# One written order for all engines of an attention and MoE kernel, with the first unit's MoE in plain float32

## The chip, the cores and the metric

The kernel runs on one core of a Trainium2 chip. Its engines each work through a queue of their own in order: TensorE (PE; PEld is its weight load), VectorE (DVE), ScalarE (ACT), GpSimd (POOL) and SyncE (SP), which here issues all transfers. The metric is the device time of one execution in microseconds; the median of three runs of the kernel before is 644.41 us.

## The reference

The reference computes a gated linear attention with a complex decay and puts its output through a dense feed-forward block with a special gate, called MoE in the code. Cut to what matters:

```python
mag = sqrt(a_re**2 + a_im**2);  scale = minimum(mag, 0.999) / (mag + 1e-6)
for t in range(768):                       # batch 4, heads 8, head_dim 48
    S = (a_re + 1j*a_im)[t] * scale[t] * S + k[t] v[t]^T     # complex state, per head
    y[t] = q[t] @ real(S)
x = y as (3072 tokens, 384)
h = x @ w_in                               # (384, 2048)
out = (h * tanh(softplus(h))) @ w_out      # (2048, 384)
```

All inputs are float32 but the two weights, which arrive as float64 and are handed to the kernel as 64-bit integers.

## The kernel before

**Units.** The 3072 tokens are cut into 12 units of 256 tokens (a batch has three), and each unit into two chunks of 128. A unit passes through three parts.

The *elementwise* part (`ew_steps`) loads a_re, a_im, q, k and v and turns the decay into a magnitude and a phase: logarithms and exponentials (function table "natural_log_exp"), arctangent, sine and cosine (table "trig"), two prefix sums, the growth of q and k, and their rotation. Units 0 and 1 are worked in halves. The rotated q and k are sent through the DMA queues into another layout, the tile `T` (24 transfers for a unit, called relays).

The *attention* part (`attn_steps`) does for each chunk and each group of four heads: transposes of k (`pkn`, L462), products of k and q (`pa`, L470), masked on VectorE (`am`, L473), the output (`ypsum`, L486, with the chunk's own values and with the old state), and the state's update (`pd`, L502; addition L508; fade on POOL, L510, for unit 0 on VectorE). The output is moved into the layout `xf` by four transfers. These matmuls are plain float32.

The *MoE* part (`moe_steps`) works in eight pairs of 128-column blocks. For pair j, `mm1` makes `ph` = x w_in (L548), then a chain runs: exponential (ScalarE), cap (VectorE, L553), square, logarithm, exponential (ScalarE), gate (VectorE, L558), the split of the gate's result `g` into `gh` and `gl` (L157, L158), and `mm2` adds g w_out to `po` (L576). In float32 precision this is done with float32r products: each operand is split into a high and a low part, and a product is three matmuls (high x high, low x high, high x low). There are three `ph` buffers, so TensorE can be three pairs ahead of the gate.

**Weights.** `win` and `wout` convert the float64 words in 24 pieces of 512 words: ScalarE scales the low word (L123 on `raw` and `wraw`), VectorE shifts and joins the high word (L190, L194), POOL adds the carry (L199), and the split makes high and low parts (L157, L158). All this must be done for a piece before any product uses it. Since the weights come late, the MoE of units 0 and 1 is halved: pairs 0 to 3 of unit 0, pairs 0 to 3 of unit 1, then pairs 4 to 7 of each. The first half's sums go to a buffer in memory (`held`) and come back.

**Order.** Each step is put on a time line by tables of constants (`EW`, `AT`, `WP`, `LD` and others) and the framework's scheduler orders the instructions by the resulting priorities and by its own time simulation. Table loads of ScalarE are kept together by added dependencies (`with_trig`): one excursion to the trig table for units 0 and 1, two for each later unit. Thirty bf16 matmuls on `junk` keep TensorE occupied before the first products (L434).

Of the kernel before, what the change touches and what calls it, by code (L numbers as in the profile page):

```python
# [33 lines left out]
NJ = 3  # L34
DJ = D // NJ
W = TU + NCH
NPAIR = DF // (2 * P)
LAG = 3
TB = 3
HACT, HMOD = 2, 3  # L40
LDVE, LMOD = 6, 6
GACT = 0
GATE = -1
GRP = 2
RG, QG, GN = 3, 1, 0
SQ0, SORD, CGA, CGN, CGD, ACTG = 1, 0, 3, 3, 0, 0
YDVE = []
RQ = [(), ()]
LG, WG = 12, 12
W1 = 0  # L50
ADDV = 12
CLAMPP, MAGP = 0, 0
ROTU = 2
ROTP = [2]
TREE = 1
WXB, WRB, WI = 1, 2, 512
FIN0 = -2.63
FS = 0.0
TRUNC = 0
AFTERX = 0  # L60
NUN = 12
SUBP = 0
MULP = 0
LONG = 2
WIDE = 1
WREP, WREP2, WK = 18, 12, -8.6
FAST = [0, 1]
EW = [(-16.11, -10.98), (-12.73, -8.83), (-13.6, -11.78), (-17.88, -11.79), (-16.43, -10.6)]
AT = [(-7.62, -4.55), (-3.79, -0.81), (-8.05, -2.82), (-8.41, -3.06), (-10.49, -2.73)]
WP = [(-7.98, -3.4), (-2.82, 2.46), (1.94, 7.2), (9.3, 9.35)]  # L70
WS = [-3.58, -1.77, 0.11, 1.02]
ES = [3.85, -0.77, -2.02, 1.25]
TS = [0.08, -1.31, 2.46, -0.05]
MB = [-1.35, -0.14]
WL1 = -0.98
RB = 2
XB = 2
LD = [(-17.86, -17.24, -16.49), (-18.78, -19.85, -19.81), (-17.97, -17.71, -17.6), (-21.23, -15.07, -17.56), (-24.18, -15.85, -17.38)]
WL = 512
# [3 lines left out]
TWOPI_LO = 6.283185  # L83


@with_exitstack
def tile_kernel(ctx, tc, q, k, v, are, aim, w_in, w_out, out):
# [8 lines left out]
    ps = ctx.enter_context(tc.tile_pool(name="ps", bufs=1, space=PSUM))  # L96

# [17 lines left out]

    NOSYNC = mybir.DependencyInfo(mybir.DependencyClass.NoSync, mybir.DependencyReason.DATA)
    fence = {"last": None, "since": []}

    def after(ins, prev):
        tc.add_manual_dep(ins.ins, prev.ins.name, NOSYNC, reason="activation table order")  # L120

    def act(out, in_, func, **kw):
        ins = nc.scalar.activation(out, in_, func, **kw)  # L123
        if func in (AF.Exp, AF.Ln):
            if fence["last"] is not None:
                after(ins, fence["last"])
            fence["since"].append(ins)
        return ins

    def act_set(name, prevs):  # L130
        ins = nc.scalar.preload_act_table_set(name)  # L131
        for p in prevs:
            after(ins, p)
        return ins

    def with_trig(*parts):
        prev = act_set("trig_and_small", fence["since"] + [fence["last"]])
        for part in parts:
            if callable(part):
                part()  # L140
                continue
            for out, in_, func, kw in part:
                ins = nc.scalar.activation(out, in_, func, **kw)
                after(ins, prev)
                trig.append(ins)
                prev = ins
        fence["last"] = act_set("natural_log_exp_and_others", [prev])
        fence["since"] = []

    fence["last"] = act_set("natural_log_exp_and_others", [])  # L150

    wi = {p: wts.tile([P, NPAIR, NJ, 256], F32R, name=f"wi{p}") for p in "HL"}
    wo = {}
    raw_in = [wts.tile([P, NJ * DF // 2], I64, tag=f"wo{i}", name=f"raw{i}") for i in range(2)]

    def split(src, h, lo, heng, leng):
        heng(h, src)  # L157
        leng(out=lo, in0=src, in1=h.bitcast(F32), op=ALU.subtract)  # L158

# [3 lines left out]
    relayed = []  # L163
    placed = []
    relayed1 = []
    qloads = []
    turned = []
    converted = []
    trig = []
    rotated = []  # L170

    def load_win(half):
        def f():
            for o in range(0, NJ * DF // 2, WL):
                ins = nc.sync.dma_start(raw_in[half][:, o:o + WL],
                                        w_in[:, half * NJ * DF // 2 + o:half * NJ * DF // 2 + o + WL])
                if half:
                    after(ins, placed[3] if o // WL >= RG else qloads[-1] if QG else relayed[-1])
        return f

    def convert(n, raw, dst, ws, raw_is_in=False):
        u = raw.bitcast(U32).rearrange("p (n two) -> p n two", two=2)
        lo, hi = u[:, :, 0], u[:, :, 1]
        if not TRUNC:
            ins = act(lo.bitcast(I32), lo, AF.Copy, scale=2.0 ** -29)
            if CGA < 9:
                after(ins, trig[0 if len(converted) < CGN else CGA])
            converted.append(ins)
        x = me.tile([P, ws], U32, tag="wx", name="wx", bufs=WXB)
        first = nc.vector.tensor_scalar(x, hi, 3, 0x3FFFFFF8, ALU.logical_shift_left, ALU.bitwise_and)  # L190
        after(first, turned[1] if n < GN and raw_is_in else turned[GATE])
        if CGD:
            after(first, rotated[CGD - 1])
        nc.vector.scalar_tensor_tensor(hi, hi, 0xC0000000, x, ALU.bitwise_and, ALU.bitwise_or)  # L194
        if TRUNC:
            nc.vector.scalar_tensor_tensor(hi, lo, 29, hi, ALU.logical_shift_right, ALU.bitwise_or)
        else:
            hi, lo = hi.bitcast(I32), lo.bitcast(I32)
            nc.gpsimd.tensor_tensor(hi, hi, lo, ALU.add)  # L199
        split(hi.bitcast(F32), dst[0], dst[1], nc.scalar.copy if n % HMOD < HACT else nc.vector.tensor_copy,  # L200
              (nc.vector if n % LMOD < LDVE else nc.gpsimd).tensor_tensor)

    HALF = NJ * DF // 2

    def win(n):
        def f():
            half, o = divmod(n * WI, HALF)
            dst = [wi[p].rearrange("p a b c -> p (a b c)")[:, n * WI:(n + 1) * WI] for p in "HL"]
            convert(n, raw_in[half][:, o:o + WI], dst, WI, True)
        return f  # L210

    def wout(n):
        def f():
            half, o = divmod(n * WI, HALF)
            if o == 0:
                wo[half] = wts.tile([P, 2, DF // P // 2, DM], F32R, tag=f"wo{half}", name=f"wo{half}")
            raw = me.tile([P, WI], I64, tag="wraw", name="wraw", bufs=WRB)
            ins = nc.sync.dma_start(raw, w_out[:, n * WI:(n + 1) * WI])
            after(ins, placed[3] if AFTERX > 1 else relayed[-1])
            if WG < 12:  # L220
                after(ins, relayed1[WG])
            dst = [wo[half][:, i].rearrange("p a b -> p (a b)")[:, o:o + WI] for i in range(2)]
            convert(n, raw, dst, WI)
        return f

    good = const.tile([P, UNITS + GRP, 3], F32, name="good")
    ncar = const.tile([P, NJ], F32, name="ncar")
    units = {}

    def ew_steps(u):  # L230
        b, uu = divmod(u, NU)
        st = units[u] = {}
        pool = nc.vector if u < ADDV else nc.gpsimd
        groups = range(NCH) if u < GRP else (slice(0, NCH),)
        F = NJ * TU
        T4 = [P, NCH, NJ, C]
        X5 = [P, NCH, NJ, 2, C + 1]

        def load_a():
            for n in "RI":  # L240
                if u == 0:
                    st[n] = at.tile(T4, F32, tag={"R": "xH", "I": "xL"}[n], name=f"{n}0", bufs=2)
                else:
                    st[n] = io.tile(T4, F32, tag=n, name=n, bufs=RB)
            for g in groups if u == 0 else (slice(0, NCH),):
                for n, src in (("R", are), ("I", aim)):
                    ins = nc.sync.dma_start(flat(st[n], g), src[u].rearrange("p (c j t) -> p c j t", c=NCH, t=C)[:, g]
                                      if isinstance(g, int) else src[u].rearrange("p (a t) -> p a t", t=C))
                    if u == 2 and LG < 12:
                        after(ins, relayed1[LG])  # L250

        def load_q():
            st["QK"] = io.tile(X5, F32, tag="QK", name="QK", bufs=1)
            for a, src in ((0, q), (1, k)):
                ins = nc.sync.dma_start(st["QK"][:, :, :, a, :C].rearrange("p c j t -> p (c j) t"),
                                  src[u].rearrange("p (a t) -> p a t", t=C))
                if u == 1:
                    qloads.append(ins)

        def load_v():  # L260
            st["V"] = io.tile([P, NCH, DM], F32, tag="V", name="V", bufs=2)
            ins = nc.sync.dma_start(st["V"], v[u])
            if u == 2 and LG < 12:
                after(ins, relayed1[LG])

# [4 lines left out]
        def part(x, g):  # L270
            return flat(x, g)[:, :, :C]
# [7 lines left out]
        def line(x):  # L279
            return x.rearrange("p a t -> p (a t)")  # L280
# [536 lines left out]
```

## Time and profile before

| | |
|---|---|
| three runs | 644.46, 644.41, 643.52 us |
| median | 644.41 us |
| profiled execution, first to last instruction | 645.8 us; no device time of its own is listed beside this span |
| busy: TensorE, VectorE, ScalarE, POOL | 583.5, 500.8, 490.7, 119.9 us |
| first split product of the MoE (L548) | 53.4 us |
| ScalarE table loads | 45, 57.7 us |

Busy time is the time in which at least one instruction of the engine was running. A group's mean duration is that of one instruction, and neighbours on an engine overlap a little. Matmuls are pipelined, so one that lasts 280 ns can be followed by the next after 118 ns; the pitch, not the duration, tells what a matmul costs.

### The profile page before, as it was taken

Reading aid. Unit: us, or ns where it says so; the run is one execution under the profiler, and the core shown is the slowest. Engines: PE = TensorE matmul, PEld = TensorE weight load, DVE = VectorE, ACT = ScalarE, POOL = GpSimd, SP = SyncE. Lnnn points to the kernel's source line nnn. Section 1 sums busy time; section 2 is a strip of 40 time slices with the busy share of each in tenths; the row PEclk is TensorE's granted clock in tenths of the full one; section 3 lists DMA queues with packets and bytes.
Section 4 is the critical chain, followed back from the end, with each engine's and each line's share of the span. In section 5 each row is a group of like instructions: output and inputs, shape, how many; then the busy total and the mean of one; then the engine's idle time right before and its main releaser. Section 6 shows DMA issues by size and latency. Waiting matters only on the chain.

```text
span 645.8 us, 11762 instructions
## 1 busy us (share of the span) xinstructions
PE 583.5 (90%) x4480; PEld 554.0 (86%) x4480; DVE 500.8 (78%) x877; ACT 490.7 (76%) x785; POOL 119.9 (19%) x99
## 2 busy tenths in 40 slices
PE   0698975888699989999999999999999999999996
PEld 0386854877699989999999999999999999999995
DVE  6989899899769869859868867977788796644551
ACT  6966977677686987977988977888898878655561
POOL 2323446326203003003003003003021030000000
PEclk9956988798899999999999999999999999999999
DMA  8859533612930450450540620711712503101000
GB/s 301 264 184 247 162 115 106 176 38 75 239 103 25 119 154 1 130 141 13 134 125 25 173 75 26 197 50 53 192 28 70 152 5 101 46 25 26 1 26 29
DMA packets 58528, 67.05 MB, mean 104 GB/s; under 512 B 4960, under 2 KB 51040, under 8 KB 58464
## 3 DMA queue, kind: packets, MB, share of 16 engines
q1 hardware_dynamic: 58464, 66.23, 35.9%
q8 instruction: 37, 0.61, 0.4%
q14 instruction: 27, 0.22, 0.1%
HBM read 36.96 MB, written 5.51 MB: 66 GB/s over the span
## 4 chain that ended last, share of the span: by engine, by line
PE 68%; DVE 12%; DMA 7%; issue 4%; POOL 3%; ACT 3%; SPq 2%; POOLq 0%; DVEq 0%
PE po L576 26%; PE ph L548 24%; PE pa L470 6%; PE ypsum L486 6%; PE pd L502 3%; DMA T<-QK 2%; PE pkn L462 2%; DVE wx L190 1%; DMA raw<-w_in 1%; POOL raw L199 1%; DMA R<-a_re 1%; DMA wraw<-w_out 1%; ACT e L123 1%; DVE e L553 1%; SPq L388 1%
## 5 line engine op out<-in xcount | busy, mean ns | idle before, releaser
L576 PE MATMUL po<-wo,gh 128*128 128x384 f32 x768 | 220.8, 348 | 11.3 <-DVE wo L157 7.4
L548 PE MATMUL ph<-xH,wiH 128*128 128x256 f32 x576 | 167.7, 293 | 6.2 <-DVE g L558 5.6
L548 PE MATMUL ph<-xL,wiH 128*128 128x256 f32 x576 | 166.9, 290 | 5.2 <-DVE xL L158 5.2
L548 PE MATMUL ph<-xH,wiL 128*128 128x256 f32 x576 | 166.6, 289 | 0.0
L123 ACT ACTIVATE e<-e 128x512 f32<-128x512 f32 x192 | 119.9, 630 | 52.8 <-DVE e L553 51.1
L576 PEld LDWEIGHTS po<-wo,gh 128*128 128x128 f32 x768 | 142.0, 190 | 16.9 <-DVE wo L157 7.7
L576 PE MATMUL po<-wo,gl 128*128 128x384 f32 x384 | 131.6, 343 | 0.0
L548 PEld LDWEIGHTS ph<-xH,wiH 128*128 128x128 f32 x576 | 112.3, 196 | 9.4 <-DVE g L558 6.0
L548 PEld LDWEIGHTS ph<-xL,wiH 128*128 128x128 f32 x576 | 113.0, 196 | 6.4 <-DVE xL L158 6.4
L548 PEld LDWEIGHTS ph<-xH,wiL 128*128 128x128 f32 x576 | 112.7, 196 | 0.0
L558 DVE SCALAR_TENSOR_TENSOR g<-e,ph 128x512 f32<-128x512 f32 x96 | 65.4, 681 | 25.5 <-ACT e L123 24.9
L553 DVE TENSOR_SCALAR e<-e 128x512 f32<-128x512 f32 x96 | 58.1, 605 | 32.9 <-ACT e L123 32.7
L123 ACT ACTIVATE e<-ph 128x512 f32<-128x512 f32 x96 | 56.8, 593 | 28.7 <-PE ph L548 28.2
L576 PEld LDWEIGHTS po<-wo,gl 128*128 128x128 f32 x384 | 73.1, 190 | 0.4 <-issue 0.4
L510 POOL TENSOR_TENSOR S<-S,T 96x384 f32<-96x384 f32 x18 | 23.0, 1279 | 266.4 <-DVE S L508 113.9
L158 DVE TENSOR_TENSOR gl<-g,gh 128x512 fp32r<-128x512 f32 x96 | 70.8, 737 | 1.6
L123 ACT ACTIVATE e<-e,fifth 128x512 f32<-128x512 f32 x96 | 69.2, 721 | 1.8
L157 DVE CAST gh<-g 128x512 fp32r<-128x512 f32 x96 | 41.4, 432 | 35.1 <-PE po L576 33.5
L375 POOL TENSOR_TENSOR QK<-QK,X 128x1536 f32<-128x1536 f32 (+1 forms) x12 | 40.2, 3353 | 103.2 <-ACT X L123 90.7
L131 ACT ACT_TABLE_LOAD x45 | 57.7, 1283 | 1.6 <-PEq L773 0.8
L470 PE MATMUL pa<-T 96*128 96x128 f32 x384 | 52.0, 287 | 0.0
L470 PEld LDWEIGHTS pa<-T 96*128 96x128 f32 x384 | 48.9, 201 | 0.9 <-issue 0.7
(88 smaller groups left out, 826.2 us busy)
## 6 DMA issues: line engine op xcount, KB each, us to landing
T<-X SPq DMA_DIRECT2D x72, 129.0 KB, 2.5
T<-QK SPq DMA_DIRECT2D x72, 129.0 KB, 3.8
raw<-w_in SPq DMA_DIRECT2D x12, 512.0 KB, 8.3
wraw<-w_out SPq DMA_DIRECT2D x12, 512.0 KB, 3.7
QK<-q SPq DMA_DIRECT2D x12, 384.0 KB, 3.9
QK<-k SPq DMA_DIRECT2D x12, 384.0 KB, 5.0
V<-v SPq DMA_DIRECT2D x12, 384.0 KB, 4.3
out_dram<-o SPq DMA_DIRECT2D x24, 192.0 KB, 1.9
```

What stands on the lines that cost most here:

```text
L123: ins = nc.scalar.activation(out, in_, func, **kw)
L131: ins = nc.scalar.preload_act_table_set(name)
L157: heng(h, src)
L158: leng(out=lo, in0=src, in1=h.bitcast(F32), op=ALU.subtract)
L375: (nc.vector if g in FAST and u == 0 else nc.gpsimd).tensor_tensor(QK[..., :C], QK[..., :C], X[..., :C], ALU.mult)
L470: nc.tensor.matmul(pa[:, i, :], st["T"][c][:, 4 * g + i, 1, :C], st["T"][c][:, 4 * g + i, 0, :C], start=True, stop=True)
L486: nc.tensor.matmul(py[64 * par:64 * par + D, i, :], lhs, rhs, start=n == 0, stop=first or n == 1)
L510: (nc.vector if u < WIDE else nc.gpsimd).tensor_tensor(nS, nS, pe, ALU.mult)
L548: nc.tensor.matmul(ph[:, a, :], wi[wp][:, j, kt, a * P:a * P + P], st[xp][:, kt, :], start=n == 0, stop=n == 8)
L553: nc.vector.tensor_scalar_min(e, e, math.exp(20.0))
L558: nc.vector.scalar_tensor_tensor(g, e, 2.5, ph, ALU.subtract, ALU.mult)
L576: nc.tensor.matmul(po[t], gp[:, a, tsl], wo[part][:, wp, 2 * i + a, :], start=j in starts and a == 0 and n == 0, stop=j + 1 in ends and a ...
```

## The change

The scheduler and its tables of constants go. The kernel records 2417 operations in a list, each with its name and the engines that may do it, and then issues them in an order that is written out by hand as a list of numbers (`ORDER`); a letter behind a number names an engine other than the first allowed. Each engine's queue gets its instructions in this order, and the function table is loaded where the order makes it necessary.

```diff
+ORDER = [(int(x.rstrip("VAGTS")), x.lstrip("0123456789")) for x in """
+0 2 3 1 6 285 5 7 27 286 538 8 4 10 30 121 11 9 126 13 16 289 12 537 28 14 17 31 29 19 18 33 36 20 15 32 21 34 22 24
...
+class Work:
...
+    def act(self, out, in_, func, **kw):
+        need = TABLE.get(func)
+        if need and need != self.table:
+            self.nc.scalar.preload_act_table_set(need)
+            self.table = need
+        return self.nc.scalar.activation(out, in_, func, **kw)
+
+    def issue(self, tc):
+        order = ORDER or [(i, "") for i in range(len(self.ops))]
...
+        for i, other in order:
+            engines, name, f = self.ops[i]
+            e = other or engines[0]
```

The weights come in 16 pieces of 768 words (`WC`), one of w_in and one of w_out for each pair. A piece is first made a plain float32 tile `w`; its split into `wh` and `wl` is a second step (`halves`), which writes `wl` into the place of the piece before.

```diff
+    def weight(i):
+        src = (w_in, w_out)[i % 2][i // 2]
...
+        op("S", f"w{i} load", load)
+        op("A", f"w{i} low", low)
+        op("V", f"w{i} shift", shift)
+        op("V", f"w{i} join", join)
+        op("GV", f"w{i} carry", carry)
+
+    def halves(i):
+        def high(e):
+            if i < NW - 2:
+                wh[i] = wts.tile([P, WC], F32R, tag=f"w{NW + i}", name="wh")
+                wl[i] = None
...
+        def rest(e):
+            if wl[i] is None:
+                wl[i] = wts.tile([P, WC], F32R, tag=f"w{i - 1 if i else 2 * NW - 2}", name="wl")
+            e.tensor_tensor(wl[i], w[i], wh[i].bitcast(F32), ALU.subtract)
+
+        op("AV", f"w{i} high", high)
+        op("V", f"w{i} rest", rest)
```

Unit 0's MoE (`plain`) multiplies x and w as plain float32, one product in place of three, without a split of x, g or the weights. No unit's MoE is halved; `held`, its transfers and its additions are gone.

```diff
-    def moe_steps(st, row0, unit=UNITS, cut=False, act=act):
-        starts, ends = ((0, NPAIR // 2), (NPAIR // 2, NPAIR)) if cut else ((0,), (NPAIR,))
+    def moe(u, st, row0, op=op, act=act, plain=False):
...
+                terms = [(w, "x")] if plain else [(wh, "xH"), (wh, "xL"), (wl, "xH")]
...
+                terms = [(g_[j], w)] if plain else [(gs[j][0], wh), (gs[j][1], wh), (gs[j][0], wl)]
...
+            if not plain:
+                op("VA", f"{n} gh", high(j))
+                op("V", f"{n} gl", rest(j))
```

The work is spread over the engines differently. The growth of q and k, the size, the slope and the state's fade may be on VectorE or POOL; in the order 13 growths are on VectorE and one on POOL, and of 20 fades nine are on POOL, all from unit 4 on. Four of the 16 carries are on VectorE. Thirty of the 88 `gh` casts are on ScalarE, where all 96 were on VectorE. Some evictions (`kn out`, `y out`, `xH`, `o`), all on ScalarE before, are on VectorE. The rotation is one instruction for q and k together (`turn sin`, `turn cos`), where it was two. There are 63 table loads in the order where 45 stood. 24 junk matmuls stand in the order where 30 stood.

Two neighbourhoods of the order matter later. On SP, the load of piece 13 stands right ahead of the last of unit 1's four input moves, and pieces are loaded into two `words` buffers. On TensorE, unit 1's first product stands behind unit 0's last `mm1` and ahead of its last `mm2`; from unit 1 on, each unit's first three or four `mm1` stand among the `mm2` of the unit before.

More of the change, by code (lines that the diff above doesn't have):

```diff
@@ L114, in tile_kernel @@
     nc.gpsimd.memset(fifth, 0.2)
[L116 to L158, printed above, removed]
+    good = const.tile([P, UNITS + SPLIT_UNITS, 3], F32, name="good")
+    ncar = const.tile([P, NJ], F32, name="ncar")
@@ L181, in convert @@
[L181 to L224, printed above, removed]
@@ L252, in load_q @@
[L252 to L264, printed above, removed]
+        TX = [P, NJ, TU]
@@ new lines, in chunk, with move, f @@
+            for g in range(2):
+                op("T", f"{n} y{g}", y(g))
+            op("AV", f"{n} y out", y_out)
+            if not last:
+                for g in range(2):
+                    op("T", f"{n} pd{g}", pd(g))
+                    op("V", f"{n} S add{g}", add(g))
+                op("VG", f"{n} S fade", fade)
+        for c in range(NCH):
+            chunk(c)
+        def move(p0, j, r0, n):
+            def f(e):
+                e.dma_start(st["x"][p0:p0 + 4 * n, j, :], st["y"][r0:r0 + n].rearrange("r i t -> r (i t)"))
+            return f
@@ new lines, in attention, with high, f, rest @@
+        for r, run in enumerate(XRUNS):
+            op("S", f"u{u} x move{r}", move(*run))
+        if u < PLAIN:
+            return
+        def high(j):
+            def f(e):
+                (e.copy if e is nc.scalar else e.tensor_copy)(st["xH"][:, j], st["x"][:, j])
+            return f
+        def rest(j):
+            def f(e):
+                e.tensor_tensor(st["xL"][:, j], st["x"][:, j], st["xH"][:, j].bitcast(F32), ALU.subtract)
+            return f
+        for j in range(NJ):
+            op("AV", f"u{u} xH{j}", high(j))
+            op("V", f"u{u} xL{j}", rest(j))
@@ L642, in tile_kernel, with general @@
     nc.gpsimd.memset(ones, 1.0)
-    nc.vector.tensor_scalar(good[:, :, 1], good[:, :, 1], HIGH, None, ALU.is_le)
-    nc.vector.tensor_reduce(total, good.rearrange("p u k -> p (u k)"), mybir.AxisListType.X, ALU.add)
-    pt = ps.tile([P, 4, C], F32, tag="pa", name="ptotal", bufs=2)
-    nc.tensor.matmul(pt[:1, 0, 0:1], total, ones, start=True, stop=True)
-    want = float(P * (UNITS * (NJ * TU + 1 + NJ * NCH) + GRP))
-    nc.vector.tensor_scalar(okay, pt[:1, 0, 0:1], want, None, ALU.is_equal)
+    end = {}
+    for u in range(UNITS):
+        elementwise(u)
+        attention(u)
+        if u == 0:
+            for _ in range(SPINS):
+                op("T", "spin", spin)
+        if u == 0:
+            for i in range(NW):
+                weight(i)
+        if u == PLAIN:
+            for i in range(NW):
+                halves(i)
+        if u + 1 == UNITS:
+            verdict()
+        moe(u, units[u], u * TU, plain=u < PLAIN)
+    with tc.manual_schedule():
+        op.issue(tc)
     flag = nc.values_load(okay[0:1, 0:1], min_val=0, max_val=1)
     with tc.If(flag < 1):
-        general(tc, nc, q, k, v, are, aim, dict(io=io, ew=ew, at=at, ps=ps, dram=dram), moe_steps, split)
-def general(tc, nc, q, k, v, are, aim, pools, moe_steps, split):
+        general(tc, nc, q, k, v, are, aim, dict(io=io, ew=ew, at=at, ps=ps, dram=dram), moe,
+                lambda engines, name, f: f(op.engines[engines[0]]))
+def general(tc, nc, q, k, v, are, aim, pools, moe, now):
     io, ew, at, ps, dram = (pools[n] for n in ("io", "ew", "at", "ps", "dram"))
@@ L762, in general @@
             sl = slice(c * P, (c + 1) * P)
[L763 to L769 removed]
+            nc.scalar.copy(st["xH"][:, :, sl], px)
+            nc.vector.tensor_tensor(st["xL"][:, :, sl], px, st["xH"][:, :, sl].bitcast(F32), ALU.subtract)
+        moe(UNITS, st, u * TU, op=now, act=nc.scalar.activation)
 def build(nc_run=True):
```

818 lines of the change are left out of this document (429 added, 389 removed), and 13 rows, old and new, of the table ORDER.

## The prediction

> **What bounds the kernel now.** I read the page first, then the busy time by stretches.
>
> ```profile
> span 645.8 us, 11762 instructions
> ...
> PE 583.5 (90%) x4480; PEld 554.0 (86%) x4480; DVE 500.8 (78%) x877; ACT 490.7 (76%) x785; POOL 119.9 (19%) x99
> ...
> PEclk9956988798899999999999999999999999999999
> ```
>
> TensorE is busy 90% of the span, but the clock row shows that a good part of the loss lies in the first eleven slices (176 us). I cut the span where unit 3 starts its first product and where unit 8 does: a unit has 144 instructions on L548, so these are numbers 432 and 1152 of that line. The columns are start:end, length, busy time (count) of PE and PEld, granted clock, DMA share, GB/s; first L548, then L576.
>
> ```profile
> 0.00:227.70 227.70, 66.57 (x432) 62.77 (x432) 0.87 0.52 155
> 227.70:457.70 230.00, 97.41 (x720) 91.27 (x720) 1.00 0.34 93
> 457.70:640.00 182.30, 77.44 (x578) 73.09 (x576) 1.00 0.20 54
> ...
> 227.70:457.70 230.00, 94.91 (x477) 81.44 (x476) 1.00 0.34 93
> 457.70:640.00 182.30, 86.85 (x444) 76.31 (x444) 1.00 0.20 54
> ```
>
> The same stretches for all engines (PE, PEld, DVE, ACT, POOL), and two pieces of the first one:
>
> ```profile
> 0.00:227.70 227.70, 174.91 (x1215) 157.91 (x1216) 201.00 (x358) 172.57 (x286) 75.83 (x65) 0.87 0.52 155
> 227.70:457.70 230.00, 227.46 (x1853) 219.45 (x1852) 184.35 (x311) 192.05 (x300) 29.67 (x23) 1.00 0.34 93
> 457.70:640.00 182.30, 181.18 (x1416) 176.66 (x1414) 115.45 (x210) 125.97 (x201) 14.43 (x11) 1.00 0.20 54
> ...
> 48.00:128.00 80.00, 60.66 (x397) 52.27 (x396) 75.32 (x125) 58.92 (x96) 36.04 (x22) 0.80 0.56 159
> 128.00:176.00 48.00, 36.41 (x273) 34.69 (x272) 42.30 (x71) 34.80 (x52) 18.80 (x11) 0.93 0.44 119
> ```
>
> So there are two kernels in one. Until 228 us VectorE sets the pace (75.32 of 80 us, 94%, between 48 and 128) and TensorE waits at a lowered clock. After that TensorE is 99% busy, with ScalarE at 83% (192.05 of 230) and VectorE at 80%.
>
> The pitch of TensorE comes from the chain of waits and the timeline, as one group's start to the next one's:
>
> ```profile
> 592.60 2.12 PE ph L548 x18
> 594.72 2.12 PE po L576 x12
> ...
> 65.70 1.95 PE L470 MATMUL pa<-T 96*128 96x128 f32 x16
> 67.41 0.36 PE L548 MATMUL ph<-xH,wiL 128*128 128x256 f32 x1
> ...
> 69.02 0.39 PE L486 MATMUL ypsum<-T,S 96*48 96x128 f32 x4
> 69.25 0.39 PE L486 MATMUL ypsum<-am,V 128*48 128x128 f32 x4
> ```
>
> A split product takes 118 ns on L548 (256 columns) and 177 ns on L576 (384). A plain float32 product appears as two instructions; in attention's L470 each takes (67.41-65.70)/16 = 107 ns for 128 columns. Attention's other form goes every 57 ns.
>
> **The change, part by part.** *Unit 0 in plain float32.* It removes 144 + 96 split instructions (8 x 2.12 + 8 x 2.12 = 33.9 us) and puts 48 + 32 plain products, each two instructions, in their place. At L470's 107 ns per 128 columns these take 96 x 0.214 + 64 x 0.321 = 41.0 us, so TensorE gets 7.1 us more. If they went at the split products' pitch it would be 96 x 0.118 + 64 x 0.177 = 22.7 us (11.2 less); at half clock 82 us (48 more). I take 41.0, the same kind of instruction. Unit 0 loses its eight gh/gl pairs and its x split, and the weights' split (a copy and a subtraction a piece) moves behind the piece's first use.
>
> *The halved MoE.* Four evictions, eight transfers of 192 KB and four additions go. They lie beside other work; I give them no time. Their cover is the first stretch's VectorE bound.
>
> *Weights.* 16 pieces of 768 words in place of 24 of 512: the same bytes and elements, fewer fixed costs. 16 load issues stand in the order on SP where 24 stood. One hazard: unit 1's last input move stands right behind the load of piece 13, which waits until piece 11 has left one of the two `words` buffers; unit 1's first products and the relays of unit 2 queue behind it. Between the two places the order gives TensorE 16 us of unit 0's products and attention, which hide the wait, so I cost it at nothing; whatever the load is later than these 16 us would be bare.
>
> *POOL.* Twelve carries, nine fades, one growth, one size and one slope stay; the other growths and the state fades of the early units go to VectorE. Why that need not cost VectorE:
>
> ```profile
> 95.51 4.19 POOL L375 TENSOR_TENSOR QK<-QK,X 128x1536 f32<-128x1536 f32 x1
> ...
> 96.29 3.70 DVE L190 TENSOR_SCALAR wx<-raw 128x512 uint32<-128x512 uint32 x1
> ...
> L553 DVE TENSOR_SCALAR e<-e x96: 407/426/2853, 64.2 to 629.3; 128x512 f32<-128x512 f32 x96
> L553 DVE TENSOR_SCALAR e<-e 128x512 f32<-128x512 f32 x96 | 58.1, 605 | 32.9 <-ACT e L123 32.7
> ...
> L306 DVE TENSOR_TENSOR I<-I,X 128x768 f32<-128x768 f32 x10 | 9.5, 950 | 0.0
> L306 DVE TENSOR_TENSOR I<-I,X 128x384 f32<-128x384 f32 x4 | 2.2, 552 | 0.0
> ```
>
> A 0.4 us shift took 3.70 us and ended with POOL's growth (99.70 and 99.99); the cap has a median of 426 ns and a mean of 605, so 96 x 0.179 = 17 us of VectorE's busy time is waiting inside the instruction. The added growths have 1536 elements: 0.95 us for 768 and 0.40 more for each further 384 make 1.75 us, ten times, 17.5 in all, about what the shorter caps give back. By its own count along the order VectorE stays near 494 us and is no longer the first bound.
>
> *ScalarE.* This is where the change costs. Thirty of the 96 gh casts go to ScalarE, and the order makes it switch its function table 63 times, not 45.
>
> ```profile
> L123 ACT ACTIVATE e<-e 128x512 f32<-128x512 f32 x192 | 119.9, 630 | 52.8 <-DVE e L553 51.1
> L123 ACT ACTIVATE e<-e,fifth 128x512 f32<-128x512 f32 x96 | 69.2, 721 | 1.8
> L123 ACT ACTIVATE e<-ph 128x512 f32<-128x512 f32 x96 | 56.8, 593 | 28.7 <-PE ph L548 28.2
> L131 ACT ACT_TABLE_LOAD x45 | 57.7, 1283 | 1.6 <-PEq L773 0.8
> L157 ACT CAST wiH<-raw 128x512 fp32r<-128x512 f32 x8 | 5.3, 664 | 2.1 <-POOL raw L199 2.1
> L123 ACT ACTIVATE X<-X 128x768 f32<-128x768 f32 x30 | 25.5, 849 | 0.1
> L123 ACT ACTIVATE X<-X,tiny 128x768 f32<-128x768 f32 x20 | 18.7, 935 | 3.4 <-DVE X L302 3.4
> ```
>
> A round of a MoE pair is 2 x 0.630 + 0.721 + 0.593 = 2.574 us. The groups' means add up to 527 us against the page's 490.7, so two neighbours overlap by 36.5/785 = 0.047 us, which I take off each instruction but the loads. Counting the order ahead of unit 3's first product: 28 table loads (35.9), 23 rounds (59.2), 31 conversions of weights of 768 words at about 1.0 (30), the halves of units 0 and 1 (four times 7.1), later units' elementwise passes (47 at 0.85 to 1.03, 41.6) and copies (17); 289 instructions, 212.6 - 261 x 0.047 = 200.3 us. Up to unit 8's first product: 31 loads (39.8), 40.5 rounds (104.2), 14 casts (9.3), 79 elementwise passes (69.7), copies (18.3); 327 instructions, 241.3 - 296 x 0.047 = 227.4 us. Before, these two stretches held 172.57 and 192.05.
>
> [...] In the trace a load starts at 13.91 and the next activation at 15.21, so a switch costs 1.30 us, and 18 more cost 23.
>
> ```profile
> 13.91 1.28 ACT L131 ACT_TABLE_LOAD   x1
> 15.21 0.52 ACT L143 ACTIVATE I<-I 128x384 f32<-128x384 f32 x1
> ```
>
> [...]
>
> *TensorE in the order.* Unit 3 to unit 8: 720 instructions on L548 as before, 468 on L576 (9 fewer), 708 of attention against 1853 - 720 - 477 = 656. At 0.177 and 0.08 us (between 57 and 107 ns) that is 230 - 1.6 + 4.2 = 232.6 us. From unit 8 to the end: 2 fewer on L548, 24 fewer on L576, 62 fewer of attention: 182.3 - 0.2 - 4.2 - 5.0 = 172.9 us.
>
> *The sum.* An engine that sets the pace was 94% busy above; I give ScalarE 95%, since it shares no wait with POOL. First stretch 0.8 + 200.3/0.95 = 211.6 (TensorE needs less, below); second the larger of 232.6 and 227.4/0.95 = 239.4; third 172.9 for TensorE, ScalarE having only 103 us left; then 645.8 - 640.0 = 5.8 as before, for the last copies and stores. That is 629.7 us of span against 645.8. The profiled span stands 1.4 us above the median 644.41, so the forecast is **628.3 us**. Its own range is ScalarE shares of 93 to 97%, 619 to 638.
>
> **The rivals.** *TensorE keeps its own pace (faster still).* If the ScalarE work fits beside, the first stretch is 0.8 + 200.3 (no idle at all), the second 232.6: 201.1 + 232.6 + 172.9 + 5.8 - 1.4 = 611.0. For it: the second stretch ran 99% before. Against: ScalarE would have to be busy 98% for 230 us.
>
> *ScalarE's queue becomes the bound and loses time at its head (slower).* Its instructions run in order; with 66 a unit in place of 60 between units 3 and 8, an exponential stands behind a table load or a pass whose input is late, three `ph` buffers fill, and TensorE stops. In the first stretch before, the pace setter VectorE was busy only 201.0/227.7 = 88%. With that share: 0.8 + 427.7/0.88 + 172.9 + 5.8 - 1.4 = 664. It is slower than before from a share below 427.7/(645.8 - 0.8 - 172.9 - 5.8) = 91.7%. For it: nothing has slack any more, since VectorE, by its own count, has 208 of these 240 us to do and TensorE 233.
>
> *The clock.* The first stretch holds 155 us of TensorE work at full clock (6 x 4 warm-up products, unit 0's 41.0, the rest by the pitches), and attention starts at about 29 us, since 26 us of ScalarE's work stand ahead of it in the order.
>
> ```profile
> 32.00:48.00 16.00, 15.98 (x105) 14.26 (x103) 13.01 (x28) 9.88 (x19) 4.49 (x6) 0.50 0.56 193
> ```
>
> The clock was 0.50 there, 0.80 and 0.93 in the two pieces above. At 0.93 TensorE needs 29 + 155/0.93 = 196 us, less than ScalarE; at 0.75 it is 236, 24 more than my sum: 652. From 0.78 on down the gain is gone. [...]
>
> *No change at all* would need the two effects to cancel.
>
> **How the numbers follow.** Forecast 0.46; TensorE's pace 0.24; the ScalarE queue 0.20; the clock 0.06; cancelling 0.04. The range runs from below the second case (608, if the overheads of the later stretches shrink a little too) to 652, between the forecast and the slow cases; under 0.2 is left outside. About 0.2% is what a measurement of this kernel tells from no change. Faster 0.70, same 0.04, slower 0.26.
>
> **What would show it.** Right: L548's instruction 432 near 212 us and 1152 near 451, ScalarE over 93% busy between, 63 table loads of 1.28 us, VectorE's cap with a mean near its median, unit 0's plain instructions at 0.21 and 0.32 us. Wrong: TensorE over 98% busy from 130 us on (then the second case), ScalarE's busy share under 92% while TensorE waits for g (the third), a granted clock under 0.8 until 200 us (the fourth), or SP standing at piece 13's load while unit 1's products wait.

## The result and the profile after

The changed kernel takes 626.26 us (median of four runs, 623.0 to 627.56) against 644.43 us, a ratio of 0.9704 with a 95% interval of 0.9669 to 0.9739. The forecast was 628.3 us. The time came out 2 us below it, but not by the way that was forecast, as the stretches show. Executions more than 1.5% longer than the fastest of the same kernel are left out of the ratios; that removes two, both of the experiment that leaves products out.

The page of the kernel after, its span, busy times and clock row:

```profile
span 621.3 us, 11450 instructions
...
PE 568.6 (92%) x4394; PEld 532.8 (86%) x4394; DVE 482.2 (78%) x836; ACT 507.4 (82%) x804; POOL 42.9 (7%) x38
...
PEclk9998999799999999999999999999999999999999
```

POOL's busy time fell from 119.9 to 42.9 us, ScalarE's rose by 17, VectorE's fell by 19, and the clock's early hole is smaller: up to unit 3 half clock is on record for 13.7 us here and for 61.4 us before. The early clock has to be read with care. This trace's record of the clock begins at 33.4 us, and where there is no record the views print 1.00; TensorE's first 16 products of `pa`, at 28.67 us, take 3.67 us, and the next 16, at 36.89 us, take 1.98, so the first went at half clock. This execution took 623.0 us itself, so 1.7 us lie around its span; the four runs had spans of 621.3 to 625.8 us.

Busy time by stretches, cut where unit 3 and unit 8 start their first product (the kernel after has 96 instructions on its product line for unit 0, so these are numbers 385 and 1105) and at the last product; columns as in the prediction (PE, PEld, DVE, ACT, POOL, clock). First after, then before at the same events:

```profile
0.00:210.65 210.65, 166.99 (x1168) 142.24 (x1169) 191.02 (x319) 188.95 (x296) 27.21 (x26) 0.97 0.56 166
210.65:442.15 231.50, 228.43 (x1881) 220.94 (x1880) 197.56 (x341) 214.27 (x332) 12.18 (x8) 1.00 0.36 101
442.15:615.50 173.35, 173.14 (x1349) 169.64 (x1348) 93.14 (x177) 104.21 (x178) 3.48 (x4) 1.00 0.14 38
```

```profile
0.00:229.00 229.00, 176.21 (x1223) 159.21 (x1224) 202.25 (x360) 173.81 (x288) 75.83 (x65) 0.87 0.53 156
229.00:460.90 231.90, 229.35 (x1863) 221.35 (x1862) 185.54 (x313) 193.81 (x303) 29.67 (x23) 1.00 0.34 95
460.90:640.00 179.10, 177.98 (x1397) 173.46 (x1396) 113.03 (x204) 122.98 (x196) 14.43 (x11) 1.00 0.19 51
```

| stretch | before | forecast | after |
|---|---|---|---|
| to unit 3 | 229.0 | 211.6 (ScalarE) | 210.65 |
| to unit 8 | 231.9 | 239.4 (ScalarE; TensorE alone 232.6) | 231.5 |
| to the last product | 179.1 | 172.9 (TensorE) | 173.35 |
| tail | 5.8 | 5.8 | 5.8 |

Between the two profiles the gain is 24.5 us: 18.4 in the first stretch, 0.4 in the second, 5.8 in the third. (The profiled execution of before was a long one of its kind and this a short one; the medians differ by 18 us.) One term of the forecast is off, the second, by 8 us.

Windows of 16 us of the kernel after, same columns:

```profile
16.00:32.00 16.00, 4.64 (x24) 4.67 (x24) 15.56 (x38) 15.66 (x29) 1.05 (x1) 1.00 0.39 121
32.00:48.00 16.00, 10.90 (x106) 9.58 (x105) 15.93 (x24) 15.87 (x26) 4.91 (x3) 0.86 0.79 241
...
64.00:80.00 16.00, 14.96 (x95) 10.74 (x94) 14.17 (x24) 15.60 (x24) 4.47 (x3) 1.00 0.76 222
80.00:96.00 16.00, 13.50 (x84) 9.83 (x84) 16.00 (x23) 14.70 (x24) 4.44 (x2) 1.00 0.54 185
...
112.00:128.00 16.00, 15.29 (x106) 11.91 (x105) 11.72 (x18) 12.04 (x20) 2.42 (x1) 0.90 0.47 127
128.00:144.00 16.00, 16.00 (x107) 14.27 (x108) 15.72 (x28) 15.18 (x25) 0.00 (x0) 1.00 0.07 26
...
226.00:242.00 16.00, 16.00 (x138) 15.89 (x136) 15.67 (x28) 15.91 (x25) 0.00 (x0) 1.00 0.61 174
...
290.00:306.00 16.00, 16.00 (x122) 15.65 (x121) 13.38 (x27) 15.95 (x29) 0.00 (x0) 1.00 0.52 149
```

Until about 112 us VectorE is as full as ScalarE, or fuller (16.00 of 16 from 80 to 96), but for the window from 64 to 80, and TensorE has gaps. From about 120 us on TensorE is full: from 130 us to its last product it is busy 482.1 of 485.4 us. And from 226 to 306 us ScalarE keeps up beside it at 15.9 of 16 us.

Groups of the kernel after that answer to steps of the prediction (busy us, mean ns, idle before):

```profile
L164 ACT ACT_TABLE_LOAD x63 | 80.8, 1283 | 1.1
L627 ACT CAST gh<-g 128x512 fp32r<-128x512 f32 x30 | 18.4, 616 | 9.7 <-PE po L644 7.2 <-DVE g L621 2.4
...
L668 DVE TENSOR_SCALAR e<-e 128x512 f32<-128x512 f32 x96 | 42.5, 443 | 36.2 <-ACT e L166 35.7
L423 DVE TENSOR_TENSOR QK<-QK,X 128x1536 f32<-128x1536 f32 x9 | 15.8, 1756 | 4.3 <-DMA QK<-q 3.5 <-ACT X L166 0.5 <-DMA QK<-k 0.4
L429 DVE COPY QK<-X 128x12 f32<-128x12 f32 x5 | 0.9, 174 | 0.9 <-DMA T<-QK 0.9
```

### The profile page after: what moved, and what is told of

The parts are those of the page before. It is cut to its first block, busy times and chain, and to the rows that moved or that the text cites. A ratio compares the mean times of both kernels' runs of the same rounds, so it can differ in the third digit from the quotient of the medians.

```text
span 621.3 us, 11450 instructions
## 1 busy us (share of the span) xinstructions
PE 568.6 (92%) x4394; PEld 532.8 (86%) x4394; DVE 482.2 (78%) x836; ACT 507.4 (82%) x804; POOL 42.9 (7%) x38
## 4 chain that ended last, share of the span: by engine, by line
PE 38%; ACT 31%; DVE 15%; DMA 8%; issue 4%; SPq 3%; DVEq 0%; ACTq 0%
PE ph L609 15%; PE po L644 14%; ACT e L166 10%; ACT X L166 7%; ACT L164 6%; PE pa L509 3%; PE ypsum L527 3%; DMA T<-QK 3%; DMA x<-y 2%; DVE g L621 2%; SPq L454 2%; PE pd L539 2%; ACT R L166 2%; DMA I<-a_im 1%; DVE gl L633 1%
## 5 line engine op out<-in xcount | busy, mean ns | idle before, releaser
L609 PE MATMUL ph<-xH,wh 128*128 128x256 f32 x462 | 134.6, 291 | 1.7 <-DVE g L621 1.6
L609 PE MATMUL ph<-xL,wh 128*128 128x256 f32 x462 | 130.1, 281 | 0.0
L609 PE MATMUL ph<-xH,wl 128*128 128x256 f32 x462 | 129.8, 281 | 0.0
L644 PE MATMUL po<-wh,gh 128*128 128x384 f32 x308 | 106.7, 347 | 0.0
L644 PE MATMUL po<-wh,gl 128*128 128x384 f32 x308 | 104.7, 340 | 0.5 <-DVE gl L633 0.5
L644 PE MATMUL po<-wl,gh 128*128 128x384 f32 x308 | 104.3, 338 | 0.0
L609 PEld LDWEIGHTS ph<-xH,wh 128*128 128x128 f32 x462 | 87.2, 189 | 5.3 <-issue 1.7
L609 PEld LDWEIGHTS ph<-xL,wh 128*128 128x128 f32 x462 | 87.1, 189 | 0.2
L609 PEld LDWEIGHTS ph<-xH,wl 128*128 128x128 f32 x462 | 87.2, 189 | 0.0
L164 ACT ACT_TABLE_LOAD x63 | 80.8, 1283 | 1.1
L644 PEld LDWEIGHTS po<-wh,gh 128*128 128x128 f32 x308 | 57.9, 188 | 1.5 <-issue 1.5
```

The source lines that it names most:

```text
L164: self.nc.scalar.preload_act_table_set(need)
L609: e.matmul(ph[j][:, a, :], win(x, j, kt, a), st[y][:, kt, :], start=n == 0, stop=n + 1 == len(todo))
L644: e.matmul(po[t], x[:, a, t * P:(t + 1) * P], wout(y, j, a), start=j == 0 and a == 0 and n == 0, stop=j + 1 == NPAIR and a == 1 and n + 1 ...
```

## The experiments

All twelve are compared with the kernel before, run beside them. The changed kernel itself was measured three times (0.9704, 0.9754, 0.9721; the third is the edit below that changed nothing), mean 0.973, 627 to 628 us at the before of these runs; single results of one kernel thus scatter by 0.3%, 2 us, and differences are given against that mean.

**The changed kernel again.** 

> The changed kernel unchanged, as the base for the runs beside it: about 623 to 627 us, with stretches of 210.6, 231.4, 173.5 and 5.8 us as in its first profile (cut at unit 3's and unit 8's first product and at the last product).

It took 627.48 us against 644.36, 0.9754 (0.9732 to 0.9776); in its profile unit 3 starts at 211.0 and unit 8 at 443.2 us.

**Less work for ScalarE.**

```diff
-            e = other or engines[0]
+            e = "V" if name.endswith(" gh") else other or engines[0]
```

> All 30 gh casts that the order gives to ScalarE go to VectorE (14 of them between unit 3's and unit 8's first products, one before, 15 behind). The prediction's theory, ScalarE sets the pace up to unit 8: 15 casts of 0.616 us at 95% are worth 9.7 us, so the kernel is about 9 to 10 us faster than the changed one. The rival, TensorE sets the pace from about 116 us on to the end and ScalarE has slack: within 1.5 us of the changed kernel, or slower by what VectorE's later gh delays.

626.29 us, 0.972 (0.9695 to 0.9745): no change. The second stretch of this kernel:

```profile
214.60:446.70 232.10, 228.77 (x1881) 220.91 (x1880) 202.51 (x356) 207.84 (x318) 12.30 (x8) 1.00 0.36 101
```

ScalarE has 6.4 us less to do and the stretch is as long as ever. ScalarE does not set its length.

**Less work for TensorE.** The products with the low part of the weights are left out in unit 5.

```diff
-                terms = [(w, "x")] if plain else [(wh, "xH"), (wh, "xL"), (wl, "xH")]
+                terms = [(w, "x")] if plain else [(wh, "xH"), (wh, "xL"), (wl, "xH")][:2 if u == 5 else 3]
-                terms = [(g_[j], w)] if plain else [(gs[j][0], wh), (gs[j][1], wh), (gs[j][0], wl)]
+                terms = [(g_[j], w)] if plain else [(gs[j][0], wh), (gs[j][1], wh), (gs[j][0], wl)][:2 if u == 5 else 3]
```

> Leaves out the products with the low part of the weights in unit 5: 48 products of 0.118 us and 32 of 0.177 us, 11.3 us of TensorE's work in the second stretch; ScalarE's and VectorE's work is the same. ScalarE sets the pace: no change, within 1.5 us. TensorE sets the pace: up to 11.3 us faster, and less by as much as ScalarE, which is 99% busy from 224 to 304 us, cannot follow; 6 to 11.

621.99 us (median of six), 0.9629 (0.959 to 0.9669): 5 us faster by the medians of all executions, 6.5 by the ratio. Its second stretch:

```profile
211.60:438.25 226.65, 220.34 (x1801) 210.90 (x1800) 200.49 (x341) 212.52 (x331) 13.55 (x8) 0.99 0.37 103
```

The stretch is 4.85 us shorter for 11.3 us of products left out: TensorE does set the pace, but something close behind it keeps the rest (ScalarE is busy 212.52 of these 226.65 us, 94%).

**More work for ScalarE, a try that did nothing.**

```diff
             self.table = need
+            self.loads += 1
+            if self.loads in range(29, 60, 2):
+                self.nc.scalar.preload_act_table_set(need)
```

> Every second function table load between unit 3's and unit 8's first products is done twice: 16 more loads of 1.283 us, 20.5 us more of ScalarE's time. ScalarE sets the pace there: 20 to 22 us slower. TensorE sets the pace, ScalarE has 17.3 of 231.4 us idle: 3 to 10 us slower, what falls into the stretches in which ScalarE has no idle time left.

627.09 us, 0.9721 (0.9694 to 0.9747). But the second load of each pair left no instruction; the trace has 63 loads as before:

```profile
L165 ACT ACT_TABLE_LOAD x63 | 80.8, 1283 | 1.1
```

So this says nothing of ScalarE. It is a third measurement of the unchanged kernel, which became useful below.

**More work for ScalarE, done.**

```diff
-                act(e_[j], ph[j], AF.Exp)
+                for _ in range(2 if 3 <= u < 8 else 1):
+                    act(e_[j], ph[j], AF.Exp)
```

> The first exponential of every pair of units 3 to 7 is done twice, with the same result: 40 more instructions of 0.59 us, about 21 us more of ScalarE's time in the second stretch (231.4 us, ScalarE busy 214). ScalarE sets the pace: 21 to 22 us slower than the changed kernel. TensorE sets the pace: slower by what does not fit into 17 us of idle time and falls into the 80 us in which ScalarE was 99% busy, 4 to 12.

643.68 us, 0.9983 (0.9955 to 1.0011): 16 us slower. The first stretch is as before (210.3 us), the second is

```profile
210.30:458.60 248.30, 234.93 (x1881) 224.05 (x1880) 197.89 (x338) 234.38 (x370) 13.59 (x8) 0.99 0.34 94
```

16.8 us longer for 20.1 us more of ScalarE's busy time. Neither theory had this: nothing to gain by 6 us less, almost all to lose by 20 us more. ScalarE is the second engine: here it is busy 234.38/248.30 = 94.4% of the stretch, all but the 95% of the prediction, and before this edit it stood at 214.27/231.5 = 92.6%, just under that. Such a share is a mean over the stretch: from 226 to 306 us ScalarE was 99% busy without the edit, so an exponential added there found no room, which is a reading of the windows and was not tested apart.

**Unit 0 split like the others.** `PLAIN = 0`, with x's split behind unit 0's moves, a `gh` and a `gl` behind each of its gates, and each piece's split some ten operations behind its carry, in the order otherwise as it was; only the products of pairs 3, 6 and 7 stand later in it, behind their piece's split.

```diff
-PLAIN = 1
+PLAIN = 0
```

> Unit 0 split like the others, with the weights' split moved ahead of its products: TensorE has 7.1 us less, VectorE some 22 us more ahead of unit 1's first product (13 weight subtractions of 0.95, eight gh/gl pairs of 1.12, three for x), ScalarE about 1 us more. ScalarE sets the early pace, as predicted: within 3 us of the changed kernel. VectorE shares it: 12 to 22 us slower. TensorE sets it: 7 us faster.

648.21 us, 1.004 (1.0018 to 1.0063): 20 us slower, and all of the change's gain is gone. To unit 1's first product, and to unit 3's:

```profile
0.00:148.40 148.40, 84.31 (x543) 71.79 (x544) 127.30 (x203) 112.23 (x177) 28.17 (x26) 0.86 0.57 176
0.00:237.10 237.10, 171.21 (x1248) 155.96 (x1249) 202.26 (x339) 191.50 (x300) 28.17 (x26) 0.91 0.49 148
```

Unit 1 starts at 148.4 us in place of 122.5, or of 127.1 in a longer execution of the changed kernel, so 21 to 26 us later, for some 22 us that VectorE has more to do ahead of it; from unit 3 on the times are the changed kernel's (229.3 us for the second stretch, 179 from there to the end). The price of plain float32, 7 us of TensorE, falls where TensorE waits anyway.

**More work for ScalarE early.**

```diff
-            (e.copy if e is nc.scalar else e.tensor_copy)(wh[i], w[i])
+            for _ in range(2 if e is nc.scalar else 1):
+                (e.copy if e is nc.scalar else e.tensor_copy)(wh[i], w[i])
```

> ScalarE's 15 casts of the weights' high parts are done twice, with the same result; 13 of them stand ahead of unit 1's first product, 10 us more of ScalarE's time there. ScalarE sets the early pace, as predicted: 10 to 12 us slower, all of it ahead of unit 1's first product. VectorE and the transfers set it, as the split unit 0 suggests: less than 5 us slower.

633.71 us, 0.9815 (0.9787 to 0.9844): 5.5 us slower, between the two; in its profile unit 1 starts at 131.5 us. 10 us of ScalarE cost about half of themselves, 22 us of VectorE cost 20 or more. This speaks for VectorE as the nearer bound of the early part, with ScalarE beside it, and does not prove it: in the split unit 0 the products wait for the split of their weights, while unit 0 of this run uses nothing that was done twice, so part of the difference can be the longer chain and not the engine.

**Without the junk matmuls.**

```diff
-SPINS, SPIN = 6, 4
+SPINS, SPIN = 6, 0
```

> Without the 24 junk matmuls. If they hold the clock up for unit 0's attention and products (granted 0.86 to 1.0 between 32 and 80 us, where the kernel before had 0.50 to 1.0) and TensorE decides there: 5 to 10 us slower, with a clock near 0.5 somewhere between 32 and 80 us. If ScalarE and VectorE set the pace until 116 us: within 2 us, whatever the clock does.

628.64 us, 0.9712 (0.9675 to 0.9749): no change. Its early windows, columns as above:

```profile
32.00:48.00 16.00, 15.13 (x100) 13.99 (x101) 15.64 (x23) 15.74 (x26) 4.97 (x3) 1.00 0.78 237
48.00:64.00 16.00, 11.33 (x63) 9.27 (x60) 14.88 (x25) 13.71 (x20) 3.72 (x2) 1.00 0.75 211
```

The windows print a clock of 1.00, but TensorE's rows contradict them (start, length):

```profile
28.72 3.67 PE L509 MATMUL pa<-T 96*128 96x128 f32 x16
...
57.00 4.06 PE L609 MATMUL ph<-x,w 128*128 128x256 f32 x12
...
61.25 0.39 PE L527 MATMUL ypsum<-am,V 128*48 128x128 f32 x4
```

Sixteen products of `pa` take 3.67 us (2.06 at full clock), and the first plain products, from 57 us, take 4.06 for twelve instructions (2.83 at 103.57 us in the changed kernel's profile). This trace's record of the clock begins at 59.6 us, and 1.00 is printed for the time ahead of it. So without the junk TensorE works at half clock from its first product at 27 us to 59.6 us, as the first branch of the expectation had it, but without that branch's 5 to 10 us: the clock does not decide there. That the missing junk is the reason for the late clock is not shown, since in the changed kernel's first profile full clock is on record from 33.4 to 43.6 us (16 products of `pd` take 1.56 us at 34.81 there, 2.69 at half clock in the kernel before), ahead of the first junk at 48.24. The changed kernel, too, shows that the early clock does not decide: up to 51 us it has some 13 us of half clock in its first profile and some 20 in its second, and unit 1 starts at 122.5 and 122.6 us.

**The growths back on POOL.**

```diff
-            e = other or engines[0]
+            e = "G" if name.endswith(" grow") and "a " not in name and "b " not in name else other or engines[0]
```

> The growths of units 2 to 11 on POOL, as before the change (nine more there, 4.2 us each in place of 1.76 on VectorE). The prediction's term, that VectorE gives back in waits what it is relieved of: the cap's mean rises from 443 ns toward 600, VectorE's busy time falls by less than 8 of these 15.8 us; time within 3 us, since only unit 2's growth lies ahead of the point from which TensorE is full. The rival, VectorE's own work counts: 8 us or more faster.

640.93 us, 0.9897 (0.9846 to 0.9948): 11 us slower, which neither side expected. The second stretch has 10.5 of them:

```profile
217.60:459.65 242.05, 232.52 (x1880) 223.84 (x1879) 200.83 (x338) 214.61 (x333) 30.00 (x13) 0.99 0.34 97
```

One of the growths in the timeline (TensorE, VectorE and POOL; start, length, and in brackets the wait):

```profile
268.21 3.49 POOL L423 TENSOR_TENSOR QK<-QK,X 128x1536 f32<-128x1536 f32 x1 [14.00 <-ACT X L166]
268.28 3.46 DVE L429 COPY QK<-X 128x12 f32<-128x12 f32 x1
...
272.46 1.61 PE L539 MATMUL pd<-V,kn 128*96 128x48 f32 x16 [2.27 <-DVE am L516]
...
274.89 0.64 PE L527 MATMUL ypsum<-T,S 96*48 96x128 f32 x4
```

and the group of that copy:

```profile
L429 DVE COPY QK<-X 128x12 f32<-128x12 f32 x5 | 7.0, 1403 | 1.5 <-DMA T<-QK 1.5
```

A copy of twelve columns, 174 ns in the changed kernel, stands for 3.46 us until POOL's growth is done. The mask `am` stands behind it on VectorE, TensorE waits 2.27 us for `am`, and then works at half clock (0.64 us for four products of `ypsum`, 0.39 at full clock). What the prediction booked as VectorE's busy time is a wait at the head of VectorE's queue, and TensorE pays for it. Of the 10.5 us of this stretch, 6.5 are more idle time of TensorE, and 4.1 more busy time, with half clock for 6.8 us.

The expectation's other half failed too, in an instructive way. The cap's mean stays at 439 ns, and VectorE's busy time does not fall by most of 15.8 us but rises from 482.2 to 488.5. Eight of the ten growths hold some VectorE instruction for 1.9 to 3.8 us; this copy stands in the way twice, at other times it is a step of the phase or of the split of `g`, as here, where the first of two casts waits:

```profile
297.63 3.77 DVE L627 CAST gh<-g 128x512 fp32r<-128x512 f32 x2
```

So in this run the instruction that waits is the one that the order put there.

**The kernel before, with growths and fades on VectorE.** The same part of the change alone.

```diff
-            (nc.vector if g in FAST and u == 0 else nc.gpsimd).tensor_tensor(
+            nc.vector.tensor_tensor(
-                (nc.vector if u < WIDE else nc.gpsimd).tensor_tensor(nS, nS, pe, ALU.mult)
+                nc.vector.tensor_tensor(nS, nS, pe, ALU.mult)
```

> The kernel before, with all growths and fades on VectorE: 12 growths (ten of 1.75, two of 0.95 us) and about 20 fades of 0.55 us more there, some 30 us, and POOL left with the carries. The prediction's term (VectorE gets back in shorter waits what it takes over, no time): within 4 us of the kernel before. What the changed kernel with POOL's growths showed (about 1 us or more of TensorE's time lost for each growth on POOL): 5 to 12 us faster.

636.07 us against 645.62, 0.9844 (0.9816 to 0.9872): 10 us faster than the kernel before. The busy times of its page, and the cap's group:

```profile
PE 581.8 (92%) x4480; PEld 554.2 (87%) x4480; DVE 498.6 (79%) x907; ACT 491.1 (77%) x785; POOL 79.3 (12%) x69
```

```profile
L553 DVE TENSOR_SCALAR e<-e 128x512 f32<-128x512 f32 x96 | 42.0, 439 | 29.2 <-ACT e L123 29.0
```

VectorE took over some 30 us of work and its busy time fell by 2 (500.8 before). That much the prediction had right. It priced it at no time, and it is worth 10 us.

**A new order around piece 13.** In the changed kernel, TensorE, VectorE, ScalarE and SP around the load of piece 13:

```profile
101.90 0.53 SPq L249 DMA_DIRECT2D words<-w_out  x1
...
107.35 0.92 ACT L166 ACTIVATE words<-words 128x768 int32<-128x768 uint32 x1 [1.34 <-DMA words<-w_out]
...
109.03 0.68 DVE L621 SCALAR_TENSOR_TENSOR g<-e,ph 128x512 f32<-128x512 f32 x1
...
109.86 5.46 PE L644 MATMUL po<-w,g 128*128 128x384 f32 x8 [3.46 <-DVE g L621]
```

Here is also where executions of one kernel part. In the profile above unit 1 starts its first product at 122.5 us, in the third one (the doubled loads that left no instruction) at 127.1; from there to the end they take 498.8 and 499.1 us. TensorE's rows at that place, first the profile above, then the other:

```profile
115.79 0.86 PE L497 MATMUL pkn<-ident,T 96*128 96x96 f32 x8 [0.48 <-DMA T<-QK]
116.89 2.06 PE L509 MATMUL pa<-T 96*128 96x128 f32 x16 [0.24 <-ACT kn L502]
118.78 1.46 PE L644 MATMUL po<-w,g 128*128 128x384 f32 x4
```

```profile
117.44 1.42 PE L501 MATMUL pkn<-ident,T 96*128 96x96 f32 x8 [2.11 <-DMA T<-QK]
118.78 3.78 PE L513 MATMUL pa<-T 96*128 96x128 f32 x16
122.36 2.46 PE L648 MATMUL po<-w,g 128*128 128x384 f32 x4
```

Unit 2's attention starts 1.65 us later, TensorE waits 2.11 us in place of 0.48, and what follows goes at half clock. So two orders were tried that should close the gap: piece 13's scaling and shift behind pair 5's chain, unit 1's first pair ahead of unit 2's attention; its chain then has to stand ahead of that of unit 0's last pair, whose last products move behind it. The second one has eight junk matmuls ahead of unit 1's pair.

```diff
 (by name)
-w13 low, w13 shift, u0 p5 inv, w13 join, ..., u0 p5 gate
+u0 p5 inv, w13 low, ..., u0 p5 gate, w13 shift, w13 join
-u2a kn0, ..., u1 p0 mm1, ..., u0 p7 exp to gate, ..., u0 p7 mm2, ..., u1 p0 exp to gate
+u1 p0 mm1, u2a kn0, ..., u1 p0 exp to gate, ..., u0 p7 exp to gate, u0 p7 mm2
```

> A new order around 100 to 140 us: piece 13's scaling and shift stand behind pair 5's chain in place of ahead of it, and unit 1's first pair is multiplied ahead of unit 2's attention, with its chain ahead of that of unit 0's last pair. If the 3.5 us for which TensorE waits there, and the lower clock behind them, are lost for good: 2 to 6 us faster than the changed kernel, and the executions of it lie closer together. If the wait only moves to unit 2's relays: no change.

> The same order with eight junk matmuls (1.7 us) ahead of unit 1's first pair. If the clock drops because TensorE idles there, another 1 to 2 us faster than without them, with a granted clock of 1.0 between 112 and 128 us; if it drops for another reason, no change or 1 us slower.

630.4 us, 0.9763 (0.9738 to 0.9788), executions from 630.06 to 631.06, closer together, as expected; and 630.18 us, 0.9753 (0.9723 to 0.9784). Neither is faster than the changed kernel. TensorE in windows of 4 us (length, busy, clock), without the junk, and the later wait in its timeline:

```profile
116.00:120.00 4.00, 3.02 (x15) 0.62 0.89 305
120.00:124.00 4.00, 4.00 (x15) 0.52 0.01 3
...
136.00:140.00 4.00, 1.25 (x6) 0.68 0.01 4
```

```profile
138.75 0.58 PE L609 MATMUL ph<-xH,wh 128*128 128x256 f32 x1 [2.86 <-DVE g L621]
```

The same windows with the junk:

```profile
116.00:120.00 4.00, 3.62 (x27) 1.00 0.82 297
120.00:124.00 4.00, 4.00 (x23) 1.00 0.00 0
...
132.00:136.00 4.00, 0.70 (x9) 0.95 0.00 0
136.00:140.00 4.00, 3.70 (x12) 0.50 0.02 4
```

The junk did what it was to do, as far as one profile of each tells: the clock stays at 1.00 where it fell to 0.52 without it. But the late chain of unit 0's last pair now leaves TensorE without work at 136 us (2.86 us for g, and half clock after it), so the gap moved by 20 us and the gain was given back there. No version tried here beats the changed kernel.

## Why the prediction came out right

**What bounds the first stretch: right number by luck, engine in doubt.** The forecast was 211.6 us, ScalarE's 200.3 at 95%; the profiles of the changed kernel have 210.65, 211.0 and, in a longer execution, 215.8. But ScalarE had only 188.95 us to do, which at 95% is 198.9, and 10 us more of it cost 5.5. Until about 112 us VectorE is in most windows at least as near to the limit, with gaps of TensorE; from about 120 us on TensorE itself is full. The two errors, too much ScalarE work and a limit that is not ScalarE's alone, met at the same number.

**The second stretch: the term that was mis-sized.** ScalarE's work was put at 227.4 us and is 214.27. The instructions and their durations were counted well (327 and 241.3 us; by the groups of this stretch 332 and 239.6 us); what was off was the overlap of neighbours, taken as 0.047 us an instruction from the whole kernel before. In this dense stretch it is (239.6 - 214.3)/300 = 0.084 us for each instruction but the loads. Two things made the forecast's value too small. The kernel before's groups add up to 532 us, not 527, which without the 45 loads is 0.056 us an instruction. And two ScalarE instructions that touch overlap by 0.10 us in both traces, while one that starts after a wait overlaps with nothing: in the whole kernel before 419 of 740 overlap their neighbour, in this stretch 239 of 300. The first stretch has the same error: its durations add up to 209 us (212.6 forecast), but 20 us of them overlap, not 12. With the measured work the same step gives 214.27/0.95 = 225.5, less than TensorE's 232.6, and the larger of the two is TensorE's; measured 231.5. The rest of the step holds: with the doubled exponentials ScalarE's share was 94.4%. So the second stretch went as the rival in which TensorE keeps its pace, and its argument against itself, that ScalarE would have to be busy 98%, rested on the same oversized work: 92.6% was enough. The sign that the prediction gave for that rival came true, TensorE over 98% busy from 130 us on (99.3%), and its own, ScalarE over 93%, just failed. That rival's time, 611.0 us, did not come, because the first stretch took 210.65 us and not the 201.1 that it assumed.

**The third stretch and the tail** went as forecast, 172.9 and 173.35, 5.8 and 5.8. The ends of the stretches were chosen a little carelessly: the rows of before end at 227.7 and 457.7 us, behind the last product of the unit before and 1.3 and 3.2 us ahead of the first products at which the kernel after was counted. At equal cuts the same working gives 231.9 - 25 x 0.177 + 40 x 0.08 = 230.7 and 179.1 - 48 x 0.08 = 175.3 for TensorE in the two stretches, 0.8 and 2 us from the measured ones; the slip is worth no more than that.

**Time around the span.** The forecast took off 1.4 us, span of before to median. The profile of before was a long execution; the profiled execution of after was a short one, 3.3 us under its median. So the sum missed the profiled span by 8.4 us and the median by only 2.

**Unit 0 in plain float32.** The pitches were right: 0.22 and 0.32 us an instruction (0.214 and 0.321 forecast). The step said what it costs, 7.1 us of TensorE, and gave its gain no price of its own. Of the parts that were undone this one has the largest gain: without it unit 1 starts 21 to 26 us later and the time is 20 us longer, in an order that was not written anew for it.

**POOL.** VectorE's side was forecast well: the cap's mean fell to 443 ns (which alone tells little, since it is 439 with the growths back on POOL), a growth on VectorE is 1.756 us (1.75 forecast), and its busy time is 482 us, 12 under the count. The step that failed is "about what the shorter caps give back", as though a wait inside an instruction cost only the engine's busy time. It is worth 10 us in the kernel before, with the fades, and 11 in the kernel after, for nine growths. The copy of 3.46 us above ends with the growth of 3.49 us beside it (at 271.74 and 271.70 us); why the two end together is not shown.

**Table loads.** 63 of 1283 ns, as forecast, and the idle time ahead of all of them is 1.1 us. What they cost in time was not measured, since the doubled loads left none in the trace.

**Piece 13** was costed at nothing, hidden by 16 us of TensorE's work. SP issues the load at 101.90 and goes on; the cost is elsewhere. ScalarE stands 1.34 us at the piece's scaling, ahead of pair 5's last exponential, g is late, and TensorE waits 3.46 us. What this is worth in time is not shown: in the first of the new orders TensorE waits 1.07 us for that g, and the time did not fall.

**The clock** was given 0.06 for a mean of 0.75, the author's estimate, and was not the bound. The windows give 0.97 up to unit 3; with the unrecorded half clock from 27.4 to 33.4 us it is about 0.95 from TensorE's first product on. The rival's path failed too: half clock until 59.6 us, in the run without the junk, cost no time. Nor did work alone bring the full clock in the kernel before: in the row that the prediction prints, TensorE counts as busy for 15.98 of 16 us from 32 to 48 us, at a clock of 0.50.

**What stays open.** The two parts measured alone, POOL's 10 us and plain float32's 20, add up to more than the 18 of the whole change; whether they overlap or something else of it (18 more table loads, the order, the MoE that is no longer halved) takes time back isn't known. Whether VectorE alone bounds the early part isn't known either. Undoing the halving alone was not tried, since the weights' conversion would have to be placed anew with it; nor was the order as such.

## What to carry to other kernels

When a sum rests on an engine's work, take its overlap from a stretch in which that engine is dense, and compare engines by work over share: here 13 us of oversized work chose the wrong bound. Elementwise work on POOL was no free cover here (10 us in the kernel before, 11 in the kernel after): see which VectorE instructions stand behind it and who waits for them. A front in which VectorE and ScalarE prepare weights can be shortened by moving preparation behind the first use, even where TensorE pays for it (here 20 us, for 7 of TensorE's). And a clock that a view prints is worth a look at the matmuls' own durations.

## What was not expected of the hardware

In the third profile of the changed kernel a gap of 2.11 us of TensorE was followed by half clock: 3.78 us for 16 products that took 2.06 at full clock, 2.46 for four that took 1.46. With the growths back on POOL one of 2.27 us was, too: 0.64 us for four products of `ypsum` that take 0.39 at full clock. The length alone does not decide: in the profile of before, a gap of 2.17 us ends at 56.82 us and half clock is on record from 56.63 to 63.45, while one of 2.19 us ends at 156.52 and full clock is on record from 148.79 to 172.68. Up to unit 3 half clock is on record for 6.83 us twice in the changed kernel's first profile, and for 3.41 to 23.89 us at a time before. With eight junk matmuls ahead of unit 1's pair the clock is at 1.00 from 116 to 124 us in the one profile that has them, where it was 0.62 and 0.52 without them. And between the two profiles compared, unit 2's attention starts 1.65 us later, behind a transfer, and unit 1's first product 4.6 us later, nearly all of the 4.9 us between them.
